# Scores of two head groups on the two halves of TensorE's rows, a first batch attended in halves of its tokens, and casts moved towards ScalarE

## The chip, the core and the metric

The kernel runs on one core of a Trainium2 chip. The metric is the device time in microseconds, taken as the median of several runs. One core has TensorE (PE in the profile, with PEld for its weight loads), VectorE (DVE), ScalarE (ACT), GpSimd (POOL) and SyncE (SP, which issues the transfers here).

## What is computed

Eight batches of eight heads, 576 tokens, head size 64 and 32 memory slots go through a slot attention, and its output goes through two feed-forward layers of 512, 2048 and 512 columns:

```
a = softmax over tokens of phi
k_m, v_m = a^T k, a^T v
scores = q k_m^T / 8, softmax over the 32 slots
x = attn v_m, heads side by side: 4608 x 512
x = (s * relu(x w_in)^2 + b) w_out
out = (h * sigmoid(1.702 h)) w_out2 with h = x w_in2
```

## The kernel before

Each big product is three fp32r matmuls over a high and a low half (`mm3`, L259): `wh*xh`, `wh*xl`, `wl*xh`. So every operand needs a cast to its high half (`hi`, L238, on ScalarE or VectorE, lines L241 and L242 in the profile) and a subtraction for its low half (`lo` and `tt`, L244 to L251, always VectorE, line L247).

The first stage (to about 341 us) works through the batches. For a batch b:

- `slots(b, g)` for the two groups g of four heads: softmax of phi, `k_m` and `v_m` on TensorE (L439, L441), normalised (`norm`, L446) and turned into the tile `km` (L456, then a copy).
- `attend(b, g)`: the scores of one group (L481), eight matmuls into one PSUM tile. Their contraction is 64 rows, `o = slice(64*g, 64*g+64)`, so group 0 uses rows 0 to 63 of TensorE and group 1 rows 64 to 127; their outputs are four strips of 32 columns. Then on VectorE a transposition (L487), the maximum (L500), a subtraction (L490), on ScalarE the exponential (L502), on VectorE sum, reciprocal, product (L494 to L496, L490), a transposition (L505), and the halves `ah` and `al`.
- `matrix(b, j)` for four blocks j of the inner width: `v_m` times `w_in` (L524, 512 columns, both halves of the rows, tile `vw`), with its halves `mh` and `ml`. So the attention weights multiply a folded matrix.
- `step(b, pi, u)`: twelve 128x288 matmuls of `mh`, `ml` with `ah`, `al` for a half u of the tokens (L263 to L265, tile `h`), a relu (L547) and a store.

Batch 0 also converts `w_in` from 64-bit floats (`convert`, L268: five operations on VectorE and ScalarE and one on GpSimd for each of 16 tiles). Batches 2, 3, 4 and 6 carry the preparation of the next layer's weights (`prepare`). The later stages (`down` and `up`) are 8064 more matmuls of 128x288.

The order on every engine is fixed before the run by a list scheduler (`Order`, L28): each operation has a due time and one or two ways (engine, estimated cost). The scheduler takes the way whose start plus `WEIGHT` times cost is least (L115), so `WEIGHT` sets how readily a cast goes to VectorE. Engines run their lists in order. PSUM holds four tiles (`ps`) of two banks each. While `fill` is set, idle TensorE time in the plan is filled with matmuls of an identity (`warm`, L750); the second call of `warm` ends that.

Of the kernel before, what the change touches and what calls it, by code (L numbers as in the profile page):

```python
# [12 lines left out]
F32R = mybir.dt.float32r  # L13
# [5 lines left out]
P = 128  # L19
# [8 lines left out]
class Order:  # L28
# [10 lines left out]
    WEIGHT = {"dve": 1.0, "pool": 1.6, "act": 1.0}  # L39
# [113 lines left out]
class Net:  # L153
# [249 lines left out]
    def slots(self, b, g, due, lead=8):  # L403
# [42 lines left out]
        def norm():  # L446
            s = self.t(rs, [P, 1])
            nc.vector.tensor_scalar(s, T[z][:, 0, 128:129], EPS, None, op0=ALU.add)
            nc.vector.reciprocal(s, s)
            nc.vector.tensor_scalar(self.t(a, [P, P]), T[z][:, 0, 0:128], s, None, op0=ALU.mult)  # L450

        self.on_dve(d + 5, 60, norm, (z,), (a, rs), count=4)
# [10 lines left out]
    def attend(self, b, g, due):  # L463
        nc, T = self.nc, self.T
        S, J = self.S, self.S // 32
        qs = [("t", ("q", b, p)) for p in range(4)]
        if g == 0:
            for p, k in enumerate(qs):
                self.dma(due - 8 + 0.5 * p, lambda k=k: self.t(k, [P, S]), lambda p=p: self.a["q"][b, p], (), (k,))
        d = due  # L470
        ps, sm, sm2 = ((x, ("a", b, g, x)) for x in ("ps", "sm", "sm"))
        sm2 = ("sm", ("a2", b, g))
        st, aT = ("t", ("st", b, g)), ("t", ("aT", b, g))
        km, o = ("km", (b, g)), slice(64 * g, 64 * g + 64)

        def score():
            out = self.pst(ps)
            for u in range(2):
                for p in range(4):
                    w = slice(32 * p, 32 * p + 32)  # L480
                    nc.tensor.matmul(out[w, u, 0:self.HS], T[km][o, w], T[qs[p]][o, u * self.HS:(u + 1) * self.HS], start=True, stop=True)  # L481
# [7 lines left out]
        def with_slots(e, m, op):
            e.tensor_tensor(T[st], T[st], T[m].unsqueeze(2).to_broadcast([P, J, 32]), op=op)  # L490
# [6 lines left out]

        self.pe(d, 2200, score, (*qs, km), (ps,))
        self.on_dve(d + 1, self.HS, turn, (ps,), (st,), count=2)
        self.on_dve(d + 2, S, lambda: nc.vector.tensor_reduce(self.t(sm, [P, J]), T[st], axis=AX.X, op=ALU.max), (st,), (sm,))  # L500
        self.on_dve(d + 2, S, lambda: with_slots(nc.vector, sm, ALU.subtract), (sm,), (st,), port=True)
        self.on_act(d + 3, S, lambda: nc.scalar.activation(T[st], T[st], AF.Exp, scale=0.125), (), (st,))  # L502
        self.on_dve(d + 4, S + 200, total, (st,), (sm2,))
        self.on_dve(d + 4, S, lambda: with_slots(nc.vector, sm2, ALU.mult), (sm2,), (st,), port=True)
        self.on_dve(d + 5, S, lambda: nc.vector.transpose(self.t(aT, [P, S]), T[st].rearrange("p J m -> p (J m)")), (st,), (aT,))  # L505
        ah, al = ("t", ("ah", b, g)), ("t", ("al", b, g))
        self.hi(d + 6, S, lambda: self.t(ah, [P, S], F32R), lambda: T[aT], (aT,), (ah,))
        self.lo(d + 6.5, S, lambda: self.t(al, [P, S], F32R), lambda: T[aT], lambda: T[ah], (aT, ah), (al,))
# [22 lines left out]
    def step(self, b, pi, u, due):  # L531
# [13 lines left out]
        self.pe(due, 12 * HS, mm, (*m, *ats[0], *ats[1]), (h,))  # L545
# [204 lines left out]
    def warm(self, begin):  # L750
# [155 lines left out]
```

## Time and profile before

| | us |
|---|---|
| median of 3 runs (lowest, highest) | 1437.73 (1436.1, 1439.28) |
| the profiled execution, its time | 1438.46 |
| its span | 1436.4 |
| TensorE busy | 1400.5 |
| VectorE busy | 1098.2 |
| ScalarE busy | 762.4 |
| GpSimd busy | 94.7 |

The granted clock over the span is 0.992 of full speed. The time outside the span is 2.1 us. How to read it: busy time of TensorE counts pipelined matmuls as one stretch, so the space from one start to the next tells more than the duration; a row of the timeline has in brackets the idle time before it and what ended that.

### The profile page before, as it was taken

To read this page: it belongs to the slowest core of one execution; us is meant where nothing else is said; L and a number is where in the kernel's file an instruction comes from. 1 tells how busy PE (TensorE), PEld (TensorE's weight loads), DVE (VectorE), ACT (ScalarE), POOL (GpSimd) and SP (SyncE) were. 2 spreads that over 40 slices of the span, in tenths; PEclk is the share of its full clock that TensorE was granted. 3 is DMA by queue.
4 is the path that set the end of the run, shared out by engine and by line. 5 is a ranking of instruction groups with operands and counts; after the bars stand their busy time and mean duration, and the time that the engine had idled before them with its cause. 6 is when DMAs were issued, how large, how long until landed. Compare 5 with 4: busy or idle time off the path is not lost.

```text
span 1436.4 us, 28622 instructions
## 1 busy us (share of the span) xinstructions
PE 1400.5 (98%) x11190; PEld 1340.0 (93%) x11190; DVE 1098.2 (76%) x1728; ACT 762.4 (53%) x1224; POOL 94.7 (7%) x70
## 2 busy tenths in 40 slices
PE   6899999999999999999999999999999999999998
PEld 5778877789999999999999999999999999999998
DVE  7879998986898988898895565752458787777872
ACT  4455654566676666665565555554444434243441
POOL 1400110100101000100110010100000000000000
PEclk9899999999999999999999999999999999999999
DMA  9979999899954465475998756473598433554330
GB/s 354 322 258 340 353 322 344 289 309 366 313 181 131 140 238 149 156 256 171 346 347 318 278 180 239 169 266 133 188 357 310 127 116 108 156 157 131 114 104 34
DMA packets 136775, 329.19 MB, mean 229 GB/s; under 512 B 15552, under 2 KB 15552, under 8 KB 136640
## 3 DMA queue, kind: packets, MB, share of 16 engines
q1 hardware_dynamic: 136640, 327.37, 66.2%
q8 instruction: 88, 1.44, 0.4%
q14 instruction: 47, 0.39, 0.1%
HBM read 192.56 MB, written 134.74 MB: 228 GB/s over the span
## 4 chain that ended last, share of the span: by engine, by line
PE 50%; DMA 1%; DVE 0%; issue 0%; ACT 0%; SPq 0%; DVEq 0%
PE X L611 5%; PE X L613 5%; PE X L612 5%; PE X L718 5%; PE X L720 5%; PE X L719 5%; PE Y L611 3%; PE Y L613 3%; PE Y L612 3%; PE Y L718 2%; PE Y L720 2%; PE Y L719 2%; PE Z L611 1%; PE Z L613 1%; PE Z L612 1%; PE Z L718 1%
## 5 line engine op out<-in xcount | busy, mean ns | idle before, releaser
L263 PE MATMUL h<-ah,mh 128*128 128x288 f32 x512 | 160.5, 313 | 4.7 <-DVE ah L242 4.5
L265 PE MATMUL h<-ah,ml 128*128 128x288 f32 x512 | 154.3, 301 | 9.3 <-DVE ml L247 9.1
L611 PE MATMUL X<-oh,wo 128*128 128x288 f32 x512 | 152.7, 298 | 9.8 <-ACT u L637 9.7
L264 PE MATMUL h<-al,mh 128*128 128x288 f32 x512 | 154.2, 301 | 2.1 <-DVE al L247 2.1
L611 PE MATMUL X<-oh,w 128*128 128x288 f32 x512 | 151.7, 296 | 0.7 <-ACT u L631 0.7
L718 PE MATMUL X<-oh,w 128*128 128x288 f32 x512 | 151.7, 296 | 0.2 <-DMA w<-w 0.2
L612 PE MATMUL X<-ol,wo 128*128 128x288 f32 x512 | 151.6, 296 | 0.0
L719 PE MATMUL X<-ol,w 128*128 128x288 f32 x512 | 151.1, 295 | 0.3 <-DVE ol L247 0.3
L612 PE MATMUL X<-ol,w 128*128 128x288 f32 x512 | 151.0, 295 | 0.0
L613 PE MATMUL X<-oh,wo 128*128 128x288 f32 x512 | 151.0, 295 | 0.0
L720 PE MATMUL X<-oh,w 128*128 128x288 f32 x512 | 150.5, 294 | 0.0
L613 PE MATMUL X<-oh,w 128*128 128x288 f32 x512 | 150.5, 294 | 0.0
L247 DVE TENSOR_TENSOR h<-Y,u 128x576 f32<-128x576 f32 x64 | 48.4, 757 | 128.7 <-ACT u L726 89.5
L547 ACT ACTIVATE r<-h 128x576 f32<-128x576 f32 x122 | 79.5, 651 | 110.2 <-PE h L265 90.8
L263 PEld LDWEIGHTS h<-ah,mh 128*128 128x128 f32 x512 | 99.8, 195 | 26.7 <-ACT r L547 12.0
L247 DVE TENSOR_TENSOR ol<-C,oh 128x576 fp32r<-128x576 f32 x128 | 94.9, 753 | 21.5 <-ACT oh L241 11.4
L265 PEld LDWEIGHTS h<-ah,ml 128*128 128x128 f32 x512 | 99.2, 194 | 10.5 <-DVE ml L247 10.5
L241 ACT CAST oh<-A 128x576 fp32r<-128x576 f32 x106 | 68.1, 672 | 74.3 <-PE Y L613 29.8
L611 PEld LDWEIGHTS X<-oh,wo 128*128 128x128 f32 x512 | 96.2, 188 | 11.7 <-ACT u L637 11.7
L247 DVE TENSOR_TENSOR ol<-A,oh 128x576 fp32r<-128x576 f32 x128 | 94.7, 760 | 15.3 <-PE X L613 5.7
L264 PEld LDWEIGHTS h<-al,mh 128*128 128x128 f32 x512 | 99.2, 194 | 2.9 <-DVE al L247 2.9
L746 ACT ACTIVATE g<-h 128x576 f32<-128x576 f32 x96 | 65.8, 686 | 67.5 <-DVE h L247 64.4
(181 smaller groups left out, 4226.8 us busy)
## 6 DMA issues: line engine op xcount, KB each, us to landing
w<-w SPq DMA_DIRECT2D x112, 512.0 KB, 5.7
r<-r SPq DMA_DIRECT2D x128, 288.0 KB, 4.1
g<-g SPq DMA_DIRECT2D x128, 288.0 KB, 2.7
wo<-wo SPq DMA_DIRECT2D x42, 512.0 KB, 5.2
kv<-in_kv SPq DMA_DIRECT2D x64, 258.0 KB, 4.8
raw<-in_w SPq DMA_DIRECT2D x32, 512.0 KB, 6.1
q<-in_q SPq DMA_DIRECT2D x32, 288.0 KB, 4.9
A<-r SPq DMA_DIRECT2D x32, 288.0 KB, 3.2
```

The lines of the kernel that those rows point to most:

```text
L241: self.order.add(due, [self.act(n, lambda: nc.scalar.copy(out(), src()), psum), self.dve(n, lambda: nc.vector.tensor_copy(out(), src()), f ...
L247: self.order.add(due, [self.dve(n, lambda: nc.vector.tensor_tensor(out(), a(), b(), op=op), port=port)], r, w, first)
L263: self.nc.tensor.matmul(ps, wh, xh, start=start and i == 0, stop=False)
L264: self.nc.tensor.matmul(ps, wh, xl, start=False, stop=False)
L265: self.nc.tensor.matmul(ps, wl, xh, start=False, stop=(i == n - 1))
L547: self.act(2 * HS, lambda: nc.scalar.activation(self.two(r), T[h][:, :, 0:HS], AF.Relu), psum=True),
L611: nc.tensor.matmul(out, T[w][:, 0, c], T[h][:, p], start=f, stop=False, skip_group_check=True)
L612: nc.tensor.matmul(out, T[w][:, 0, c], T[l][:, p], start=False, stop=False, skip_group_check=True)
L613: nc.tensor.matmul(out, T[w][:, 1, c], T[h][:, p], start=False, stop=last, skip_group_check=True)
L718: nc.tensor.matmul(out, T[w][:, 0, c], T[h][:, k], start=f, stop=False, skip_group_check=True)
L719: nc.tensor.matmul(out, T[w][:, 0, c], T[l][:, k], start=False, stop=False, skip_group_check=True)
L720: nc.tensor.matmul(out, T[w][:, 1, c], T[h][:, k], start=False, stop=k == 1, skip_group_check=True)
```

## The change

Scores of both groups of a batch are made in one block, for each half u of the tokens into a PSUM tile of its own, with group 0 and group 1 alternating (`attend`). What follows a score is a function of its own (`weigh`), for one group and either all tokens, `(0, 1)`, or one half of them. Batch 0 is attended in two halves, each with operations of half the length; the other batches in one piece, with the two groups 4 us apart in due time and due where group 0 was. The halves `ah` and `al` get a key for each u. `matrix(0, 0)` is due 16 us sooner, and the filling of TensorE ends when its `ml` and the first half's `al` exist. `norm` leaves its last product to either engine. `WEIGHT` of VectorE goes from 1 to 2.

```diff
-    WEIGHT = {"dve": 1.0, "pool": 1.6, "act": 1.0}
+    WEIGHT = {"dve": 2.0, "pool": 1.6, "act": 1.0}
...
-            nc.vector.tensor_scalar(self.t(a, [P, P]), T[z][:, 0, 0:128], s, None, op0=ALU.mult)
-
-        self.on_dve(d + 5, 60, norm, (z,), (a, rs), count=4)
+
+        def scale(act):
+            x = self.t(a, [P, P])
+            if act:
+                nc.scalar.activation(x, T[z][:, 0, 0:128], AF.Copy, scale=T[rs])
+            else:
+                nc.vector.tensor_scalar(x, T[z][:, 0, 0:128], T[rs], None, op0=ALU.mult)
+
+        self.on_dve(d + 5, 30, norm, (z,), (rs,), count=2)
+        self.order.add(d + 5, [self.act(128, lambda: scale(True), psum=True), self.dve(190, lambda: scale(False))], (z, rs), (a,))
...
-    def attend(self, b, g, due):
+    def attend(self, b, due, groups, apart):
...
+        for n, us in enumerate(groups):
+            d = due + apart[1] * n
+            ps = {u: ("ps", ("a", b, u)) for u in us}
+
+            def score(us=us, ps=ps):
+                for u in us:
+                    out = self.pst(ps[u])
+                    for p in range(4):
+                        w = slice(32 * p, 32 * p + 32)
+                        for g in range(2):
+                            o = slice(64 * g, 64 * g + 64)
+                            nc.tensor.matmul(out[w, g, 0:HS], T[kms[g]][o, w], T[qs[p]][o, u * HS:(u + 1) * HS], start=True, stop=True)
+
+            self.pe(d, 2200 * len(us) // 2, score, (*qs, *kms), tuple(ps.values()))
+            for g in range(2):
+                self.weigh(b, g, us, ps, d, apart[0] * g)
+
+    def weigh(self, b, g, us, ps, d, later):
...
+        n = HS * len(us)
+        J = n // 32
...
+        cols = slice(us[0] * HS, us[0] * HS + n)
...
+            for i, u in enumerate(us):
+                nc.vector.transpose(x[:, i * HS:(i + 1) * HS], T[ps[u]][:, g, 0:HS])
...
+        self.on_dve(d + 1 + 0.5 * g, HS, turn, tuple(ps.values()), (st,), count=len(us))
+        d += later
+        self.on_dve(d + 2, n, lambda: nc.vector.tensor_reduce(self.t(sm, [P, J]), T[st], axis=AX.X, op=ALU.max), (st,), (sm,))
+        self.on_dve(d + 2, n, lambda: with_slots(sm, ALU.subtract), (sm,), (st,), port=True)
+        self.on_act(d + 3, n, lambda: nc.scalar.activation(T[st], T[st], AF.Exp, scale=0.125), (), (st,))
+        self.on_dve(d + 4, n + 200, total, (st,), (sm2,))
+        self.on_dve(d + 4, n, lambda: with_slots(sm2, ALU.mult), (sm2,), (st,), port=True)
+        self.on_dve(d + 5, n, lambda: nc.vector.transpose(self.t(aT, [P, n]), T[st].rearrange("p J m -> p (J m)")), (st,), (aT,))
+        self.hi(d + 6, n, lambda: part(ah), lambda: T[aT], (aT, *made(ah)), keys(ah))
+        self.lo(d + 6.5, n, lambda: part(al), lambda: T[aT], lambda: T[ah][:, cols], (aT, *keys(ah), *made(al)), keys(al))
...
-            self.pe(-5, 0, last, (x, ("t", ("al", 0, 0))))
+            self.pe(-5, 0, last, (x, ("t", ("al", 0, 1), 0), ("w", ("ml", 0, 0))))
...
-                    self.attend(0, g, -28 + 4 * g)
-                self.warm(False)
+                self.attend(0, -28, ((0,), (1,)), (2, 6))
...
-                self.matrix(b, j, d - 8)
+                self.matrix(b, j, d - (24 if b == j == 0 else 8))
+                if b == j == 0:
+                    self.warm(False)
...
-                elif b + 1 < B:
-                    self.attend(b + 1, j - 2, s0 + 18 + 7 * (j - 2))
+                elif b + 1 < B and j == 2:
+                    self.attend(b + 1, s0 + 18, ((0, 1),), (4, 0))
```

What that does to the order is seen at three places. The first is TensorE in batch 0, where `a` is a score's PSUM tile and `km` with two numbers is group 0 and group 1. Before, from the end of group 0's scores through the first half of group 1's:

```order
L481 MATMUL a_268<-q_240,km_202 32x288
L481 MATMUL a_280<-q_194,km_257 32x288
L481 MATMUL a_280<-q_210,km_257 32x288
L481 MATMUL a_280<-q_237,km_257 32x288
L481 MATMUL a_280<-q_240,km_257 32x288
```

Now, the first half of the tokens:

```order
L489 MATMUL a_269<-q_193,km_202 32x288
L489 MATMUL a_269<-q_193,km_256 32x288
L489 MATMUL a_269<-q_209,km_202 32x288
L489 MATMUL a_269<-q_209,km_256 32x288
L489 MATMUL a_269<-q_236,km_202 32x288
L489 MATMUL a_269<-q_236,km_256 32x288
L489 MATMUL a_269<-q_240,km_202 32x288
L489 MATMUL a_269<-q_240,km_256 32x288
```

Neighbours now use different halves of the rows; before, all matmuls of a group used one half.

The second is the end of batch 4's attention for group 1. On VectorE before (`st` is the weights with the slots inside, `aT` their transposition):

```order
L494 TENSOR_REDUCE a_495_2601<-st_2537 128x18
L495 TENSOR_SCALAR a_495_2601<-a_495_2601 128x18
L496 RECIPROCAL a_495_2601<-a_495_2601 128x18
L490 TENSOR_TENSOR st_2537<-st_2537,a_495_2601 128x576
L505 STREAM_TRANSPOSE aT_2612<-st_2537 128x576
L242 CAST ah_2614<-aT_2612 128x576
L247 TENSOR_TENSOR al_2616<-aT_2612,ah_2614 128x576
```

Now on VectorE:

```order
L515 TENSOR_REDUCE a_488_2599<-st_2472 128x18
L516 TENSOR_SCALAR a_488_2599<-a_488_2599 128x18
L517 RECIPROCAL a_488_2599<-a_488_2599 128x18
L511 TENSOR_TENSOR st_2472<-st_2472,a_488_2599 128x576
L537 STREAM_TRANSPOSE aT_2623<-st_2472 128x576
L247 TENSOR_TENSOR ml_2629<-vw_2543,mh_2582 128x1024
L247 TENSOR_TENSOR al_2648<-aT_2623,ah_2631 128x576
```

and on ScalarE, `r` being a step's relu:

```order
L241 CAST mh_2582<-vw_2543 128x1024
L578 ACTIVATE r_2603<-h_2561 128x576
L283 ACTIVATE cwo_2608<-raw_2513 128x512
L578 ACTIVATE r_2625<-h_2584 128x576
L241 CAST ah_2631<-aT_2623 128x576
L578 ACTIVATE r_2644<-h_2610 128x576
```

The cast `ah` went from VectorE to ScalarE, where it stands behind a relu, and an `ml` fills VectorE's list in its place. Over the whole program VectorE's list is 99 instructions shorter (1629 for 1728) and ScalarE's 119 longer (1341 for 1222). In the first stage that is, on VectorE, 12 fewer long `ah` casts, 6 fewer `mh`, 6 fewer relus, 9 fewer `km` copies and 13 fewer products in `norm`; in the later stages some 55 casts `oh`.

The third is VectorE in batch 0 after the scores of batch 1, up to the last `ml` of batch 0 (block j = 3; `an` is a maximum for batch 2's slots). Before:

```order
L413 TENSOR_REDUCE an_819<-ph_632 128x128
L490 TENSOR_TENSOR st_771<-st_771,a_812 128x576
L487 STREAM_TRANSPOSE st_844<-a_821 128x288 x2
L500 TENSOR_REDUCE a_863<-st_844 128x18
L494 TENSOR_REDUCE a_167_869<-st_771 128x18
L495 TENSOR_SCALAR a_167_869<-a_167_869 128x18
L496 RECIPROCAL a_167_869<-a_167_869 128x18
L247 TENSOR_TENSOR ml_885<-vw_835,mh_867 128x1024
```

Now:

```order
L532 TENSOR_REDUCE a_875<-st_830 128x18
L532 TENSOR_REDUCE a_878<-st_835 128x18
L511 TENSOR_TENSOR st_830<-st_830,a_875 128x576
L511 TENSOR_TENSOR st_835<-st_835,a_878 128x576
L413 TENSOR_REDUCE an_913<-ph_657 128x128
L515 TENSOR_REDUCE a_180_929<-st_830 128x18
L516 TENSOR_SCALAR a_180_929<-a_180_929 128x18
L517 RECIPROCAL a_180_929<-a_180_929 128x18
L247 TENSOR_TENSOR ml_937<-vw_902,mh_927 128x1024
```

The second group's maximum and subtraction now stand ahead of that `ml`; before, the second group's subtraction came after it.

## Rows read from the trace of the kernel before

**Rows 1.** The page's first part: busy us, share of the span, instructions.

```profile
PE 1400.5 (98%) x11190; PEld 1340.0 (93%) x11190; DVE 1098.2 (76%) x1728; ACT 762.4 (53%) x1224; POOL 94.7 (7%) x70
```

**Rows 2.** Stretches A:B: length; busy of PE, PEld, DVE, ACT, POOL; PEclk; DMA share; GB/s.

```profile
38.26:81.83 43.57, 41.18 (x372) 33.74 (x373) 38.99 (x70) 21.66 (x33) 14.93 (x11) 0.90 0.92 334
81.83:119.14 37.31, 36.91 (x375) 29.81 (x374) 29.53 (x53) 18.62 (x28) 2.61 (x2) 1.00 0.76 246
...
155.74:192.52 36.78, 36.67 (x375) 29.76 (x374) 35.61 (x63) 24.35 (x38) 5.26 (x4) 1.00 1.00 365
192.52:232.80 40.28, 38.41 (x376) 31.32 (x375) 37.49 (x67) 20.16 (x31) 5.28 (x4) 0.96 0.93 321
232.80:273.24 40.44, 38.60 (x376) 31.29 (x375) 33.17 (x57) 19.34 (x30) 2.62 (x2) 0.96 0.97 338
```

**Rows 3.** Timeline of TensorE: start, us, line, names, rows*columns, shape, count.

```profile
61.66 1.09 PE L524 MATMUL vw<-wi,km 64*32 64x512 f32 x16
62.68 1.09 PE L439 MATMUL s<-kv,ph 128*32 128x129 f32 x32
...
63.95 1.15 PE L481 MATMUL a<-q,km 64*32 64x288 f32 x16
65.03 0.40 PE L263 MATMUL h<-ah,mh 128*128 128x288 f32 x1
```

**Rows 4.** Timeline of TensorE at the start of batch 4.

```profile
195.73 0.40 PE L263 MATMUL h<-ah,mh 128*128 128x288 f32 x1 [1.47 <-DVE ah L242]
196.53 0.40 PE L264 MATMUL h<-al,mh 128*128 128x288 f32 x1 [0.40 <-DVE al L247]
...
197.50 0.44 PE L263 MATMUL h<-ah,mh 128*128 128x288 f32 x1
197.74 0.44 PE L264 MATMUL h<-al,mh 128*128 128x288 f32 x1
...
200.68 0.30 PE L265 MATMUL h<-ah,ml 128*128 128x288 f32 x1
200.81 0.30 PE L263 MATMUL h<-ah,mh 128*128 128x288 f32 x1
```

**Rows 5.** The stretch view just after that, columns as in rows 2.

```profile
196.20:200.20 4.00, 3.67 (x17) 3.67 (x18) 3.86 (x8) 0.65 (x1) 0.28 (x1) 0.60 0.94 293
```

**Rows 6.** VectorE's groups up to 345 us: count, busy us, mean ns, idle before.

```profile
L247 DVE TENSOR_TENSOR ml<-vw,mh 128x1024 fp32r<-128x1024 f32 x32 | 38.8, 1212 | 2.3 <-ACT mh L241 1.8
L490 DVE TENSOR_TENSOR st<-st,a 128x576 f32<-128x576 f32 x32 | 24.2, 758 | 0.8
...
L487 DVE STREAM_TRANSPOSE st<-a 128x288 f32<-128x288 f32 x32 | 13.5, 462 | 3.0 <-PE a L481 3.0
...
L505 DVE STREAM_TRANSPOSE aT<-st 128x576 f32<-128x576 f32 x16 | 12.4, 778 | 0.6
L247 DVE TENSOR_TENSOR al<-aT,ah 128x576 fp32r<-128x576 f32 x16 | 12.1, 757 | 0.5
L500 DVE TENSOR_REDUCE a<-st 128x18 f32<-128x576 f32 x16 | 12.0, 750 | 0.4
L494 DVE TENSOR_REDUCE a<-st 128x18 f32<-128x576 f32 x16 | 11.9, 744 | 1.1 <-ACT st L502 1.1
...
L242 DVE CAST ah<-aT 128x576 fp32r<-128x576 f32 x14 | 6.4, 459 | 0.5
```

**Rows 7.** The same of ScalarE.

```profile
L241 ACT CAST ah<-aT 128x576 fp32r<-128x576 f32 x2 | 1.3, 670 | 0.3 <-DVE aT L505 0.3
```

**Rows 8.** Timeline of VectorE in batch 0.

```profile
22.70 0.85 DVE L487 STREAM_TRANSPOSE st<-a 128x288 f32<-128x288 f32 x2 [0.71 <-PE a L481]
...
36.99 1.22 DVE L247 TENSOR_TENSOR ml<-vw,mh 128x1024 fp32r<-128x1024 f32 x1
...
74.31 1.16 DVE L247 TENSOR_TENSOR ml<-vw,mh 128x1024 fp32r<-128x1024 f32 x1
...
83.35 0.76 DVE L247 TENSOR_TENSOR al<-aT,ah 128x576 fp32r<-128x576 f32 x1
```

**Rows 9.** Timeline of TensorE in batch 0.

```profile
38.26 0.61 PE L265 MATMUL h<-ah,ml 128*128 128x288 f32 x1 [6.53 <-DVE ml L247]
...
53.07 0.40 PE L265 MATMUL h<-ah,ml 128*128 128x288 f32 x1 [2.02 <-DVE ml L247]
```

**Rows 10.** The page's costliest groups: a group of the second stage.

```profile
L611 PE MATMUL X<-oh,wo 128*128 128x288 f32 x512 | 152.7, 298 | 9.8 <-ACT u L637 9.7
```

More of the change, by code (lines that the diff above doesn't have):

```diff
@@ L460, in slots @@
         self.hi(d + 6, 128, lambda: T[km], lambda: T[tr][:, 0, 0:P], (tr,), (km,), psum=True)
-    def attend(self, b, g, due):
-        nc, T = self.nc, self.T
-        S, J = self.S, self.S // 32
+    def attend(self, b, due, groups, apart):
+        nc, T, S, HS = self.nc, self.T, self.S, self.HS
         qs = [("t", ("q", b, p)) for p in range(4)]
[L467 to L481, printed above, removed]
+        kms = [("km", (b, g)) for g in range(2)]
+        for p, k in enumerate(qs):
+            self.dma(due - 8 + 0.5 * p, lambda k=k: self.t(k, [P, S]), lambda p=p: self.a["q"][b, p], (), (k,))
+        for n, us in enumerate(groups):
[12 more added lines that the diff above has]
+                self.weigh(b, g, us, ps, d, apart[0] * g)
@@ L483, in turn @@
+    def weigh(self, b, g, us, ps, d, later):
+        nc, T, HS = self.nc, self.T, self.HS
+        n = HS * len(us)
+        J = n // 32
+        sm, sm2 = ("sm", ("a", b, g, us)), ("sm", ("a2", b, g, us))
+        st, aT = ("t", ("st", b, g, us)), ("t", ("aT", b, g, us))
+        ah, al = ("t", ("ah", b, g)), ("t", ("al", b, g))
+        cols = slice(us[0] * HS, us[0] * HS + n)
         def turn():
             x = self.t(st, [P, J, 32]).rearrange("p J m -> p (J m)")
-            for u in range(2):
-                c = slice(u * self.HS, (u + 1) * self.HS)
-                nc.vector.transpose(x[:, c], T[ps][:, u, 0:self.HS])
@@ L489, in with_slots @@
[L489 to L490 removed]
+            for i, u in enumerate(us):
+                nc.vector.transpose(x[:, i * HS:(i + 1) * HS], T[ps[u]][:, g, 0:HS])
+        def with_slots(m, op):
+            nc.vector.tensor_tensor(T[st], T[st], T[m].unsqueeze(2).to_broadcast([P, J, 32]), op=op)
         def total():
@@ L496, in total, with part, keys, made @@
             nc.vector.reciprocal(m, m)
[L498 to L508, printed above, removed]
+        def part(k):
+            if us[0] == 0:
+                self.t(k, [P, self.S], F32R)
+            return T[k][:, cols]
+        def keys(k):
+            return tuple((*k, u) for u in us)
+        def made(k):
+            return ((*k, 0),) if us[0] else ()
+        self.on_dve(d + 1 + 0.5 * g, HS, turn, tuple(ps.values()), (st,), count=len(us))
[8 more added lines that the diff above has]
+        self.lo(d + 6.5, n, lambda: part(al), lambda: T[aT], lambda: T[ah][:, cols], (aT, *keys(ah), *made(al)), keys(al))
     def matrix(self, b, j, due):
@@ L543, in mm @@
                 self.mm3(out[:, i, 0:HS], [([T[x][:, k, o] for x in m], [T[x][:, c] for x in ats[k]]) for k in range(2)])
-        self.pe(due, 12 * HS, mm, (*m, *ats[0], *ats[1]), (h,))
+        self.pe(due, 12 * HS, mm, (*m, *((*x, u) for k in ats for x in k)), (h,))
         self.order.add(due + 0.5, [
```

## The prediction

> **What bounds it now.** I read the page first: TensorE is busy 1400.5 of 1436.4 us [rows 1], so only what shortens TensorE's own list, or its waits, counts. VectorE's 76% is a mean over stages. The second view is the table of stretches, cut from the same point of one batch to the same point of the next [rows 2]. The undisturbed batches take 37.3 and 36.8 us. Two others take 40.3 and 40.4, with the granted clock down to 0.96. VectorE is busy 35.6 to 37.5 us in a batch where it also prepares weights, so there it is as long as TensorE. Batch 0 takes 43.6. The timeline at the start of batch 4 tells what the 3.5 us are: TensorE waits 1.47 us for the cast `ah` on VectorE and 0.40 for `al` [rows 4]. After that its matmuls start 0.24 us apart (197.50 to 197.74) instead of 0.13 (200.68 to 200.81), with a granted clock of 0.60 over the 4 us from 196.2 [rows 4, 5]. That is the lower of the two levels for most of them, and it loses 0.40 x 4 = 1.6 us. So a wait of 1.9 us costs 3.5.
>
> **Scores on both halves of the rows.** A group's scores are 16 instructions of 288 columns and hold TensorE from 63.95 to 65.03, 1.08 us [rows 3]; two groups take 2.16. `vw`, which already uses both halves of the rows, gets 16 instructions of 512 columns through in 1.02 us (61.66 to 62.68) [rows 3]. At its rate 32 x 288 columns take 1.02 x 9216 / 8192 = 1.15 us. So a batch saves about 1.0. The ends are 0, if alternating halves do not overlap as `vw`'s do, and 1.1, a plain halving. I take 1.0, since `vw` has the same 64-row tiles, column strips and a bank for each half. Of the eight blocks, the first lies in the start-up and batch 1's in batch 0, where VectorE sets the pace; six count: **-6.2 us** (ends 0 and -6.6).
>
> **VectorE relieved in batches 1 to 7.** Off its list go casts of 0.46 us (`ah`), six of `mh` with 1024 columns as long as `ml`'s 1.2 at most, six relus of 576 columns (about 0.76, the length of the `al` row), and short copies [rows 6]. With 20 short ones at about 0.25 that is some 10 x 0.4 + 6 x 1.1 + 6 x 0.7 + 20 x 0.25 = 20 us over seven batches, 2.8 each. VectorE's 37.5 becomes 34.7, while TensorE needs 36.8 - 1.0 = 35.8. So the excess of 3.5 and 3.6 us in batches 4 and 5 [rows 2] should mostly go. It need not all go, since the scores of both groups now come together, and all of the attention must pass VectorE before the next batch starts. By the new order that is 4 score transpositions, 2 maxima, 4 subtractions or products, 2 sums, 2 transpositions, 2 `al` and 2 `ml`: 4 x 0.46 + 2 x 0.75 + 4 x 0.76 + 2 x 0.74 + 2 x 0.78 + 2 x 0.76 + 2 x 1.21 = 13.4 us [rows 6], and up to one more us for other rows in between. TensorE has, from the scores to the next batch, seven steps of 12 x 0.13 = 1.6 and two `vw` of 1.02, 13.2 us, with about half a us for the changes between them and half a us until `al` of group 1 is read; some batches have a step or a `vw` more. These two are level, so I leave waits of 0.5 to 1 us in a few batches, some with a spell of lower clock: **-4.5 us** (ends -7.1, all gone, and 0).
>
> **The cast on ScalarE.** One `ah` takes 0.67 us there for 0.46 on VectorE [rows 6, 7]. The 0.2 us are hidden, since VectorE has the other group's rows or an `ml` to do meanwhile; without that cover two casts cost 0.4 us a batch.
>
> **The start.** The first `ml` is late today: it starts on VectorE at 36.99, and TensorE has waited 6.53 us when it goes on at 38.26 [rows 8, 9]. In the new order 28 transpositions and other short or half-length rows stand between the first transposition (22.70 before [rows 8]) and that `ml`, without the four conversion rows that stood there; I make that 12 us for 14.3, so the first steps start at 34 to 35. But what was put off comes next. To the second `al` of batch 1, at 83.35 [rows 8], VectorE ran with only 3 to 4 us of pauses in 61. The new list up to the same `al` has 112 instructions for 100: the halves add their fixed cost (two transpositions of 288 take 0.85, one of 576 takes 0.78 [rows 6, 8]), and four casts, a copy and a product get away or shorter. The sum is the same within a us. The steps of blocks 1 to 3 wait for `w_in` tiles and `ml` from this list. Then comes a wait that is new: after batch 1's scores the last `ml` of batch 0 now stands behind both groups' transpositions, maxima and subtractions and one maximum of 1.3 us. It was made at 74.31, just in time [rows 8]. By my count it stays at 75 to 76, while TensorE, without the 1.0 of scores and with no transposition between, gets there about 2 us sooner. It waits for that and may lose another 1.6 by the clock. Against it stand the wait of 2.02 at 53.07 [rows 9] and its slow matmuls, which can shrink. I take **+1 us**, with ends -5 (the earlier first steps carry through) and +3.5 (all of that new wait).
>
> **Later stages.** 8064 matmuls keep their order; 57 casts `oh` go to ScalarE. In the second stage TensorE waits 9.7 us for ScalarE's evictions of X [rows 10], and these stand in one list with the casts. I take 0, with ends -4 (the new order puts the evictions earlier) and +6. Nothing is saved there by a lighter VectorE: TensorE does not wait for it.
>
> **Sum.** -6.2 - 4.5 + 1 + 0 = -9.7. The profiled execution took 1438.46, 0.7 above the median of 1437.73. That makes 1428.8 for it, and **1428** for the median.
>
> **Rivals.**
> 1. *The early steps carry through* (the lower end of the start). For it: batch 0 takes 6.3 us more than batch 1 [rows 2], and its matmuls run partly at the lower clock. Against it: VectorE is busy 39.0 of those 43.6 us. 1428 - 6 = 1422.
> 2. *The halves do not overlap*: the scores stay at 2.16. For it: no row shows tiles of both halves in alternation. Against: `vw` [rows 3]. 1428 + 6 = 1434.
> 3. *ScalarE's casts delay the evictions.* A cast of 0.67 us ahead of an eviction is paid in full where TensorE waits for it. If one more stood before each of about nine such evictions, that is 6 us: 1434. For it: the 9.7 us of today [rows 10], which already stand for one late list. Against: the planner ranks evictions ahead. The Trainium skill, "ScalarE: Activation LUTs", section "Rules for kernel authors", says that relu, max, add and multiply belong on VectorE. The casts here agree (0.46 us there for 0.67). By that rule alone the change would be wrong wherever VectorE has room, as in the later stages.
> 4. *Slower: the joint scores choke the batch boundary.* The place is the start of batches 2 to 7. Today group 0's scores come 8 us ahead of group 1's, and half of VectorE's chain is over when the second begins. Now 13.4 us follow one point. If VectorE begins its four transpositions late by 1.5 us, behind a conversion or a maximum of its list, two of the four PSUM tiles stay full for longer and `al` comes 1.5 us after TensorE needs it; with the lower clock 3.1 us a batch. Six batches lose 18.6 instead of today's 7.1, so + 11.5 - 6.2 + 1 = + 6.3: 1444. It decides once the chain from the scores to the last `al` exceeds TensorE's 14.3 us or so. For it: the level count above. Against: 2.8 us less on VectorE in each batch. The Trainium skill, "TensorEngine Tiling (Array Packing)", section "PSUM Bottleneck", warns of this: tiles speed up TensorE but not the emptying of PSUM, which may then be the limit. No row before shows it, as no two score tiles are full together.
>
> **How the numbers follow.** My forecast has 0.60, rival 1 0.12, rival 2 0.05, rival 3 0.11, rival 4 0.12. Within 0.2% means 1434.9 to 1440.6, about what a measurement of this kernel can tell. Faster by more: the forecast almost whole (0.57), rival 1, half of rival 2 and half of rival 3, 0.77. The same: 0.03 of the forecast, the rest of rivals 2 and 3, a little of rival 4, 0.12. Slower: 0.11. The terms' own ends add up to about 1418 and 1438; I leave out the far ends of rivals 1 and 4. The range is 1418 to 1438.
>
> **What would show it.** Right: the joint score block takes 1.1 to 1.2 us; batches 2 to 7 take 36 us each, and the stretches of 40 are gone; the first step starts near 34.5, but batch 1 still starts at 82 to 85; TensorE's waits for X in the second stage remain near 10 us. Wrong: score blocks of over 2 us (rival 2), waits for `al` at every batch's start with the clock down after them (rival 4), batch 1 starting before 80 (rival 1), or waits for X of over 15 us (rival 3).

## The result, and the profile after

The changed kernel takes 1422.38 us (median of 4 runs, 1418.58 to 1423.49), the kernel before 1437.65 in the same comparison: a ratio of 0.9889 with a 95% interval of 0.9868 to 0.991. The forecast was 1428 with a range of 1418 to 1438. The profiled execution, the slowest of the four, took 1423.49 with a span of 1421.4; that is 14.97 less than the 1438.46 of the one before. Below, "the first stage ends" means the start of its last matmul in the timeline of TensorE.

The first part of the page (busy us, share of the span, instructions), to be held against [rows 1]:

```profile
PE 1389.9 (98%) x11214; PEld 1338.5 (94%) x11214; DVE 1053.8 (74%) x1629; ACT 828.5 (58%) x1343; POOL 97.2 (7%) x70
```

VectorE has 44.4 us less to do, ScalarE 66 more, TensorE 10.6 less. Next the view of stretches, cut as in [rows 2] from `vw` to `vw` (batch 0 from 38.26 on, then batches 1 to 6; columns as there):

```profile
38.26:83.00 44.74, 36.89 (x368) 28.33 (x372) 43.48 (x75) 25.30 (x41) 16.34 (x12) 0.98 0.93 330
82.95:117.98 35.03, 35.03 (x375) 29.53 (x375) 24.10 (x43) 21.54 (x34) 3.94 (x3) 1.00 0.79 264
117.98:154.59 36.61, 35.51 (x376) 29.58 (x375) 34.61 (x61) 26.84 (x44) 4.27 (x3) 1.00 0.95 330
154.59:189.55 34.96, 34.96 (x376) 29.42 (x375) 33.28 (x57) 24.21 (x40) 3.94 (x3) 1.00 1.00 376
189.55:224.46 34.91, 34.91 (x375) 29.48 (x375) 33.08 (x57) 23.22 (x38) 4.04 (x3) 1.00 1.00 360
224.46:259.43 34.97, 34.97 (x375) 29.49 (x374) 25.14 (x45) 21.06 (x34) 1.31 (x1) 1.00 1.00 356
259.43:297.50 38.07, 37.31 (x391) 31.14 (x391) 35.50 (x60) 25.81 (x43) 4.00 (x3) 1.00 0.98 344
```

Batches 3, 4 and 5 take 35.0, 34.9 and 35.0 us, where it was 36.8, 40.3 and 40.4; the clock stays at 1.00 through all of them. Batch 6 has 1.8 us of other matmuls in it, before as now. Batch 2 is the odd one, 36.6 as before. Of the kernel before, [rows 2] leaves out two of these stretches, batches 2 and 6:

```profile
119.14:155.74 36.60, 36.53 (x375) 29.78 (x374) 34.13 (x57) 22.59 (x36) 2.97 (x2) 1.00 0.97 340
273.24:312.42 39.18, 38.59 (x391) 31.50 (x390) 36.05 (x63) 21.17 (x34) 2.96 (x2) 1.00 0.79 267
```

The first stage ends at 326.35, where it was 341.27: 14.92 us, the whole of the gain. From there to the end of the last matmul it is 1091.05 us now (1417.40 less 326.35) and 1091.10 before (1432.37 less 341.27).

The scores of one batch in the timeline of TensorE (columns as in [rows 3]), with the `vw` ahead of them and the steps behind:

```profile
103.39 1.09 PE L555 MATMUL vw<-wi,km 64*32 64x512 f32 x16
104.30 1.20 PE L489 MATMUL a<-q,km 64*32 64x288 f32 x32
105.43 0.40 PE L263 MATMUL h<-ah,mh 128*128 128x288 f32 x1
105.66 0.29 PE L264 MATMUL h<-al,mh 128*128 128x288 f32 x1
105.80 0.29 PE L265 MATMUL h<-ah,ml 128*128 128x288 f32 x1
```

The two groups' block starts at 104.30 and the next step at 105.43: 1.13 us, where one group alone took 1.08 [rows 3]. Then the start of batch 4, to be held against [rows 4]:

```profile
189.55 1.09 PE L555 MATMUL vw<-wi,km 64*32 64x512 f32 x16
190.57 0.33 PE L421 MATMUL s<-ident,an 128*128 128x128 f32 x1
190.65 0.38 PE L263 MATMUL h<-ah,mh 128*128 128x288 f32 x1
190.87 0.29 PE L264 MATMUL h<-al,mh 128*128 128x288 f32 x1
191.00 0.29 PE L265 MATMUL h<-ah,ml 128*128 128x288 f32 x1
```

The start of batch 2 in the same view:

```profile
120.43 0.40 PE L263 MATMUL h<-ah,mh 128*128 128x288 f32 x1 [0.70 <-ACT ah L241]
121.22 0.40 PE L264 MATMUL h<-al,mh 128*128 128x288 f32 x1 [0.40 <-DVE al L247]
121.46 0.30 PE L265 MATMUL h<-ah,ml 128*128 128x288 f32 x1
121.59 0.29 PE L263 MATMUL h<-ah,mh 128*128 128x288 f32 x1
```

So at batch 4 nothing is left of the waits of 1.47 and 0.40: after its `vw` the steps follow 0.13 us apart. At batch 2 there are new waits, 0.70 for `ah`, which now comes from ScalarE (ACT), and 0.40 for `al`; behind them the matmuls keep their 0.13 us. Batch 6 has one wait:

```profile
261.80 0.40 PE L265 MATMUL h<-ah,ml 128*128 128x288 f32 x1 [0.76 <-DVE ml L247]
```

Before it was 0.59 at the same place, for the same tile.

The start, against [rows 9]:

```profile
31.55 0.38 PE L263 MATMUL h<-ah,mh 128*128 128x288 f32 x1
31.77 0.29 PE L264 MATMUL h<-al,mh 128*128 128x288 f32 x1
35.69 0.40 PE L265 MATMUL h<-ah,ml 128*128 128x288 f32 x1 [3.62 <-DVE ml L247]
...
47.88 1.09 PE L439 MATMUL s<-kv,ph 128*32 128x129 f32 x32 [2.24 <-ACT ph L425]
...
54.99 0.40 PE L265 MATMUL h<-ah,ml 128*128 128x288 f32 x1 [2.18 <-DVE ml L247]
...
75.28 0.40 PE L263 MATMUL h<-ah,mh 128*128 128x288 f32 x1 [0.31 <-ACT mh L241]
75.51 0.29 PE L264 MATMUL h<-al,mh 128*128 128x288 f32 x1
76.67 0.40 PE L265 MATMUL h<-ah,ml 128*128 128x288 f32 x1 [0.86 <-DVE ml L247]
```

The first step begins at 31.55 and goes on at 35.69 (38.26 before), when the first `ml`, which starts on VectorE at 34.41 (36.99 before), is there. Then come a wait of 2.24 for the exponentials `ph` of batch 1, the old wait of 2 us for `ml`, and the new one for batch 0's last `ml` after the scores of batch 1, 0.86. Batch 1 begins at 82.95, 1.1 later than before. VectorE is busy 43.5 of the 44.7 us of batch 0: it still sets the pace there.

In the later stages the page's group of [rows 10] reads now:

```profile
L642 PE MATMUL X<-oh,wo 128*128 128x288 f32 x512 | 153.3, 299 | 8.6 <-ACT u L668 8.5
```

### The profile page after: what moved, and what is told of

It is laid out like the page before. It is cut to its first block, busy times and chain, and to the rows that moved or that the text cites. A ratio compares the mean times of both kernels' runs of the same rounds, so it can differ in the third digit from the quotient of the medians.

```text
span 1421.4 us, 28723 instructions
## 1 busy us (share of the span) xinstructions
PE 1389.9 (98%) x11214; PEld 1338.5 (94%) x11214; DVE 1053.8 (74%) x1629; ACT 828.5 (58%) x1343; POOL 97.2 (7%) x70
## 4 chain that ended last, share of the span: by engine, by line
PE 91%; DVE 5%; DMA 2%; ACT 1%; issue 1%; SPq 0%; ACTq 0%; DVEq 0%
PE X L642 10%; PE X L644 9%; PE X L643 9%; PE X L749 5%; PE X L751 5%; PE X L750 5%; PE Y L642 5%; PE Y L644 5%; PE Y L643 5%; PE h L263 4%; PE h L265 4%; PE h L264 4%; PE Y L749 2%; PE Y L751 2%; PE Z L642 2%; PE Y L750 2%
## 5 line engine op out<-in xcount | busy, mean ns | idle before, releaser
L263 PE MATMUL h<-ah,mh 128*128 128x288 f32 x512 | 156.9, 306 | 1.1 <-ACT ah L241 0.7
L578 ACT ACTIVATE r<-h 128x576 f32<-128x576 f32 x128 | 83.0, 651 | 59.1 <-PE h L265 46.5
L241 ACT CAST oh<-A 128x576 fp32r<-128x576 f32 x123 | 79.9, 674 | 58.9 <-PE X L643 45.2
L241 ACT CAST oh<-C 128x576 fp32r<-128x576 f32 x115 | 76.6, 673 | 45.5 <-PE Y L643 12.7
```

The source lines that it names most:

```text
L241: self.order.add(due, [self.act(n, lambda: nc.scalar.copy(out(), src()), psum), self.dve(n, lambda: nc.vector.tensor_copy(out(), src()), f ...
L263: self.nc.tensor.matmul(ps, wh, xh, start=start and i == 0, stop=False)
L578: self.act(2 * HS, lambda: nc.scalar.activation(self.two(r), T[h][:, :, 0:HS], AF.Relu), psum=True),
```

## The experiments

All ratios are to the kernel before, measured in the same session on the same chip; "ends" is the end of the first stage in the profiled execution, and "waits for X" the idle time of TensorE in the group of [rows 10]. The rows come from five sessions, in which the kernel before took 1436.7 to 1440.1 us, so two versions are compared by their ratios and not by their medians. "Ends" and "waits" are of one execution each.

| kernel | median us | ratio, 95% interval | ends | waits for X |
|---|---|---|---|---|
| before | 1437.7 | 1 | 341.27 | 9.8 |
| the change | 1422.4 | 0.9889 [0.9868, 0.991] | 326.35 | 8.6 |
| change, WEIGHT 1 | 1435.1 | 0.9979 [0.9958, 1.0] | 339.27 | 10.0 |
| change, scores by group | 1422.7 | 0.9888 [0.9867, 0.9908] | 327.85 | 9.4 |
| before, WEIGHT 2 | 1426.9 | 0.992 [0.9898, 0.9941] | 335.59 | 7.8 |
| joint scores alone | 1431.0 | 0.9945 [0.9924, 0.9966] | 337.25 | 10.0 |
| joint scores and WEIGHT 2 | 1418.9 | 0.9876 [0.9861, 0.9892] | 327.49 | 5.8 |
| change, old start | 1418.8 | 0.9873 [0.9856, 0.989] | 326.50 | 7.5 |
| change, WEIGHT 1 later | 1423.7 | 0.9905 [0.989, 0.992] | 327.39 | 9.4 |
| change, X on VectorE | 1420.9 | 0.9881 [0.9861, 0.9901] | 327.60 | 6.8 |
| change, 4.5 us transfers | 1416.4 | 0.9854 [0.9839, 0.9868] | 325.44 | 4.4 |
| old start, 4.5 us transfers | 1413.8 | 0.9841 [0.9826, 0.9856] | 324.33 | 4.4 |
| 4.5 us, X on VectorE | 1422.6 | 0.9903 [0.9886, 0.9919] | 324.54 | 7.8 |
| old start, 4.5 us, WEIGHT 3 | 1415.4 | 0.9832 [0.9814, 0.985] | 322.87 | 5.8 |

How far one end can be trusted shows in three of the rows. The change, the change with WEIGHT 1 later and the change with X on VectorE have the same lists on TensorE, VectorE and ScalarE up to 308 us, and the first stage ends at 326.35, 327.39 and 327.60. So a difference of about 1.3 us between two ends tells nothing.

### The weight taken back

```diff
-    WEIGHT = {"dve": 2.0, "pool": 1.6, "act": 1.0}
+    WEIGHT = {"dve": 1.0, "pool": 1.6, "act": 1.0}
```

> The changed kernel with VectorE's WEIGHT back at 1 and all else kept. Theory: the waits at the start of batches 4 and 5 (3.5 us each with their slow matmuls) went because casts left VectorE; with the old weight the casts come back, the batches that prepare weights take 37 to 40 us instead of 35.0, and the time is about 1422.4 + 5 = 1427 us. Rival: the joint scores and their earlier due time took those waits away; the batches stay at 35 us and the time at 1422 us.

Measured: 1435.1 us, a ratio of 0.9979 for 0.9889; the first stage ends at 339.27, 12.9 later than with the change. The theory had the direction but less than half of the size (5 us). Without the weight, all the rest of the change keeps 2 us of the 14.9 in the first stage of the profiled execution.

### The order inside a block

```diff
-for p in range(4):
-    w = slice(32 * p, 32 * p + 32)
-    for g in range(2):
-        o = slice(64 * g, 64 * g + 64)
+for g in range(2):
+    o = slice(64 * g, 64 * g + 64)
+    for p in range(4):
+        w = slice(32 * p, 32 * p + 32)
         nc.tensor.matmul(out[w, g, 0:HS], ...)
```

> The changed kernel with the sixteen instructions of a score tile in the other order: group 0's eight and then group 1's eight, so that neighbours use the same half of the rows; nothing else moves on any engine. Theory: the halves overlap only when they alternate, so a block goes from 1.1 to 2.2 us, and seven blocks outside the start give + 7 us: 1430 us. Rival: the gain comes from one block in the place of two (fewer switches on TensorE), and the order inside does nothing: 1422 us.

Measured: 1422.7 us. The theory falls: alternation is not needed. The timelines of TensorE show why. Each row below is the start of a score block, seen through a window that closes shortly after its first instruction, so the count at its end says how many have started by then. The changed kernel, 0.06 us after the first:

```profile
104.30 0.47 PE L489 MATMUL a<-q,km 64*32 64x288 f32 x8
```

This kernel, 0.06 us after the first:

```profile
105.61 0.45 PE L489 MATMUL a<-q,km 64*32 64x288 f32 x8
```

The kernel before, 0.15 us after the first:

```profile
63.95 0.42 PE L481 MATMUL a<-q,km 64*32 64x288 f32 x4
```

In the changed kernel and in this one eight are under way at once, four strips on each half of the rows, whatever their order. Before, four are, all on one half. The gain of the pair comes from the two groups standing next to each other, which before were 6 to 9 us apart.

### The weight alone

In the kernel before:

```diff
-    WEIGHT = {"dve": 1.0, "pool": 1.6, "act": 1.0}
+    WEIGHT = {"dve": 2.0, "pool": 1.6, "act": 1.0}
```

> The kernel before with VectorE's WEIGHT at 2 and nothing else changed. Theory: VectorE's list gets shorter in the batches with preparation, the waits at the start of batches 4 and 5 go (7 us with their slow matmuls): 1437.7 - 7 = 1431 us, and the score blocks stay at 1.08 us each. Rival: the waits went through the joint scores, and the weight alone moves nothing: 1437.7 us; or ScalarE's longer list delays the evictions of X in the second stage: 1440 us.

Measured: 1426.9 us, a ratio of 0.992. The view of stretches for batches 1 to 5, cut from `vw` to `vw` (columns as above):

```profile
84.04:120.67 36.63, 36.63 (x375) 29.73 (x374) 27.93 (x50) 21.16 (x32) 2.63 (x2) 1.00 0.75 249
120.67:157.51 36.84, 36.59 (x375) 29.88 (x374) 32.52 (x57) 25.92 (x42) 5.31 (x4) 1.00 0.95 337
157.51:194.61 37.10, 36.86 (x375) 29.76 (x374) 34.48 (x61) 24.42 (x39) 3.13 (x2) 1.00 0.98 354
194.61:231.20 36.59, 36.59 (x375) 29.71 (x374) 32.72 (x58) 22.73 (x36) 5.31 (x4) 1.00 0.98 355
231.20:268.70 37.50, 36.93 (x375) 29.82 (x374) 28.75 (x50) 22.04 (x33) 1.32 (x1) 1.00 0.99 339
```

The batches of 40 are gone: all five take 36.6 to 37.5 us, with the clock at 1.00, and VectorE is busy 27.9 to 34.5 us in each. Nearly all of what remains is TensorE's own list. In the profiled execution 5.7 us come from the first stage and 4.4 from the later ones (1091.10 to 1086.72), where no term of the theory put anything; the experiment with the weight off in the later stages, below, speaks against a cause in the weight there.

### The joint scores alone

In the changed kernel, with the start of before as well (its diff stands further below):

```diff
-    WEIGHT = {"dve": 2.0, "pool": 1.6, "act": 1.0}
+    WEIGHT = {"dve": 1.0, "pool": 1.6, "act": 1.0}
...
             nc.vector.reciprocal(s, s)
+            nc.vector.tensor_scalar(self.t(a, [P, P]), T[z][:, 0, 0:128], s, None, op0=ALU.mult)
...
-        self.on_dve(d + 5, 30, norm, (z,), (rs,), count=2)
-        self.order.add(d + 5, [self.act(128, lambda: scale(True), psum=True), self.dve(190, lambda: scale(False))], (z, rs), (a,))
+        self.on_dve(d + 5, 60, norm, (z,), (a, rs), count=4)
```

> The joint scores alone: the changed kernel with WEIGHT at 1, the last product of the norm on VectorE, batch 0 attended in one piece, its first matrix due where it was, and the filling of TensorE ended as before. Theory: 1.1 us less in each score pair and some 0.4 for fewer switches, six or seven times, while VectorE is as loaded as before, so that batches 4 and 5 keep waits of 2 to 4 us each: 1437.7 - 9 = 1429 us. Rival 1: the joint order alone takes the waits away too: 1423 us. Rival 2: it chokes the batch boundary without the relief: over 1437 us.

Measured: 1431.0 us. The profiled execution was the slowest of four, 1434.7; in it the first stage ends at 337.25, 4.0 earlier than before. The same view, batches 1 to 5:

```profile
82.78:121.17 38.39, 37.03 (x376) 31.09 (x375) 29.33 (x54) 18.50 (x27) 2.68 (x2) 0.96 0.72 236
121.17:156.65 35.48, 35.27 (x376) 29.59 (x375) 34.46 (x60) 22.77 (x36) 3.01 (x2) 1.00 1.00 363
156.65:192.66 36.01, 35.62 (x375) 29.52 (x374) 34.54 (x64) 24.26 (x38) 5.33 (x4) 1.00 1.00 359
192.66:232.40 39.74, 37.15 (x375) 31.02 (x374) 37.44 (x67) 19.68 (x30) 5.25 (x4) 0.96 0.96 331
232.40:271.42 39.02, 36.77 (x375) 31.10 (x374) 33.47 (x58) 20.16 (x30) 2.86 (x2) 0.96 0.99 343
```

And TensorE's timeline at the starts of batches 4 and 5:

```profile
196.44 0.61 PE L265 MATMUL h<-ah,ml 128*128 128x288 f32 x1 [2.17 <-DVE ml L247]
...
236.20 0.40 PE L265 MATMUL h<-ah,ml 128*128 128x288 f32 x1 [2.25 <-DVE ml L247]
```

Batch 2 takes 35.5, so the saving on TensorE is there. But batches 1, 4 and 5 take 38 to 40, with the clock at 0.96; in 4 and 5 TensorE waits 2.2 us for an `ml` of VectorE, in batch 1 0.97 for `ah` and 0.40 for `al`. In this execution more than half of what the scores gave is waited away. By the medians less is lost: 1431.0 is 8.0 us below the kernel before in the same session.

### Both, and nothing else

In the kernel with the joint scores alone:

```diff
-    WEIGHT = {"dve": 1.0, "pool": 1.6, "act": 1.0}
+    WEIGHT = {"dve": 2.0, "pool": 1.6, "act": 1.0}
```

> The joint scores and WEIGHT 2 and nothing else of the change: the fourth corner beside the kernel before (ratio 1), WEIGHT 2 alone (0.992, first stage ending at 335.6 us) and the joint scores alone (0.9945, first stage ending at 337.3 us). Theory: in the first stage the two need each other, since with joint scores alone TensorE waits for VectorE and with the weight alone nothing is left but TensorE's own list; so the stage ends at 326 to 328 us, 5 us earlier than the two gains added (341.3 - 4.0 - 5.7 = 331.6), and the time is 1419 to 1422 us. Rival: the gains only add, 331.6 us, and the rest of the 14.9 us came from the norm and the split: 1426 us.

Measured: 1418.9 us, and the first stage ends at 327.49, inside the 326 to 328 of the theory. In the profiled executions the two edits alone take 5.7 and 4.0 us off the first stage, together 13.8. But the whole times say otherwise: the two ratios alone multiply to 0.992 x 0.9945 = 0.9866, and together 0.9876 [0.9861, 0.9892] was measured. By these the gains add, as near as the intervals tell. The weight is worth about the same wherever it is put in: 0.992 in the kernel before, 0.993 on top of the joint scores, 0.991 on top of the rest of the change (0.9889 over 0.9979). The profiled execution of the joint scores was the slowest of its four, the one here the fastest of its four. So it is not shown that the two edits need each other. What the norm and the split of batch 0 brought to the first stage, 1.1 us by these ends, is within the scatter.

### The start of before

```diff
-            self.pe(-5, 0, last, (x, ("t", ("al", 0, 1), 0), ("w", ("ml", 0, 0))))
+            self.pe(-5, 0, last, (x, ("t", ("al", 0, 1), 0)))
...
-                self.attend(0, -28, ((0,), (1,)), (2, 6))
+                self.attend(0, -28, ((0, 1),), (4, 0))
+                self.warm(False)
...
-                self.matrix(b, j, d - (24 if b == j == 0 else 8))
-                if b == j == 0:
-                    self.warm(False)
+                self.matrix(b, j, d - 8)
```

> The changed kernel with the start of before: batch 0 attended in one piece, its first matrix due 8 us ahead and not 24, the filling of TensorE ended by the first al. Joint scores, the norm on either engine and WEIGHT 2 stay. Theory (my forecast for the start): the split makes the first steps start 2 to 3 us earlier, but VectorE's list is the same length, so batch 1 starts at the same 82 to 85 us and the time stays at 1422 us, within 1.5. Rival: the early steps carry through, and without the split it is 4 to 5 us slower: 1427 us. Other rival: the split costs time, as the two kernels with WEIGHT 1 hint (1435.1 with it, 1431.0 without): 1418 us.

Measured: 1418.8 us, the number of the second rival. But the interval of its ratio overlaps with that of the change, so the two are not told apart. The first stage ends at 326.50, against 326.35: no difference that an end could show, so the split of batch 0 gained nothing there that can be seen. This kernel and the one with joint scores and WEIGHT 2 differ in the norm alone, and they agree too (0.9873 and 0.9876; 326.50 and 327.49). What this execution took less lies in the second stage, where one wait for X of 1.85 us with its slow matmuls is missing.

### The later stages

```diff
-                    score = t + cost * self.WEIGHT.get(eng, 1.0)
+                    score = t + cost * (1.0 if eng == "dve" and due > self.until else self.WEIGHT.get(eng, 1.0))
```

> The changed kernel with WEIGHT 2 only for what is due in the first stage, and 1 after it. Theory (term 0 for the later stages): TensorE does not wait for VectorE there, the casts can stand on either engine, and the time stays at 1422 us within 2, with TensorE's waits for the evictions of X near 9 us. Rival 1: the 57 casts on ScalarE had delayed the evictions, and without them the waits shrink: 1417 us. Rival 2: the weight alone on the kernel before brought 4 us in the later stages, and this takes them away: 1426 us.

Measured: 1423.7 us, with 9.4 us of waits for X. The casts that moved to ScalarE there cost nothing and bring nothing that can be told from the scatter.

### Evictions of X on VectorE

```diff
-nc.scalar.activation(T[k][:, o], T[X][:, o, 0:HS], AF.Identity, bias=..., scale=self.sc[:, 0:1])
+nc.vector.tensor_scalar(T[k][:, o], T[X][:, o, 0:HS], self.sc[:, 0:1], ..., op0=ALU.mult, op1=ALU.add)
...
```

The reason to try it is ScalarE's timeline in the changed kernel, just ahead of TensorE's wait of 1.85 us that ends at 646.65:

```profile
644.38 0.69 ACT L616 ACTIVATE B<-B 128x576 f32<-128x576 f32 x1 [3.80 <-DMA B<-r]
644.97 0.57 ACT L668 ACTIVATE u<-X,bw,sc 128x288 f32<-128x288 f32 x1
645.45 0.67 ACT L616 ACTIVATE D<-D 128x576 f32<-128x576 f32 x1
646.02 0.58 ACT L668 ACTIVATE u<-X,bw,sc 128x288 f32<-128x288 f32 x1
```

ScalarE stands idle for 3.80 us in front of a square whose load has not come, and the two evictions `u` that TensorE needs stand behind that square and the next one. SyncE had issued that load at 638.30:

```profile
638.30 0.32 SPq L236 DMA_DIRECT2D B<-r  x1
```

In the view of the tile `B` from 630 to 646 us its two transfers take this long from issue to landing:

```profile
DMA to landing us min/median/max: 2.8/4.4/6.1
```

So this one took about 6 us, where the plan reckons 288/340 + 2.0 = 2.85.

> The changed kernel with the second stage's evictions of X (two halves each, scale and bias) on VectorE, in the place of ScalarE. Theory: TensorE waits 8.5 us for them, and 4.4 us go at the lower clock behind those waits, because they stand on ScalarE behind squares whose loads are late (ScalarE waits 3.8 us for one load ahead of the eviction at 645 us); on VectorE they do not stand behind a load, and 5 to 10 us go: 1414 us. Rival: VectorE is 85 to 90% busy in that stage and its list waits for the same loads a little later; the waits come back as waits for VectorE: 1422 us or more.

Measured: 1420.9 us, a ratio that can't be told from that of the change. Of the 6.8 us that TensorE still waits for X, most are now for VectorE's eviction and for a cast on ScalarE. The rival was nearer.

### Transfers planned at 4.5 us

```diff
-            end[n] = t + cost + (2.0 if eng == "sync" else 0.0)
+            end[n] = t + cost + (4.5 if eng == "sync" else 0.0)
```

> The changed kernel whose planner reckons 4.5 us and not 2.0 from the issue of a transfer to its landing (the trace shows 3 to 6 us), in all stages. Theory: the planner then puts evictions of X ahead of squares whose loads have not come, and the waits of the second stage shrink by about half: 1416 us; the first stage may move by some us either way. Rival: the loads are late because SyncE's queue is held up by full tiles, and an order with later loads changes nothing there: 1422 us.

Measured: 1416.4 us. The waits for X are halved:

```profile
L642 PE MATMUL X<-oh,wo 128*128 128x288 f32 x512 | 152.8, 299 | 4.4 <-ACT u L668 4.1
```

The operations are the same, and on balance four of them went from ScalarE to VectorE (1343 to 1339, 1629 to 1633). The mechanism of the theory is seen on ScalarE: from 327 to 700 us it waits some 35 us for loads in the changed kernel and 4.5 us here. Ahead of each of the five waits for X of over 1 us in the changed kernel ScalarE waits for a load, in the 6 us before; ahead of none of the three that are left here (1.16, 1.16 and 1.74). No other value than 4.5 was tried.

### Putting them together

The start of before with 4.5 us transfers:

> The changed kernel with the start of before and with 4.5 us for a transfer in the plan, the two edits that were faster singly (1418.8 and 1416.4). Theory: the start of before was faster only because the order that followed gave one wait fewer in the second stage, and the plan with late transfers already takes that wait away: no sum, 1416 us within 2. Rival: the two add: 1412 us.

Measured: 1413.8 us, the interval of whose ratio lies wholly below that of the change: faster than the changed kernel, and than the one before. Against 4.5 us alone the intervals overlap. By ratios the two single steps would multiply to 0.9838 and 0.9841 was measured, so the rival was nearer; but neither the single gain of the old start nor its gain here is clear of the scatter. The profiled execution gained 1.1 us in the first stage and 1.5 after it against the one with 4.5 us alone.

The evictions on VectorE with 4.5 us transfers:

> The changed kernel with 4.5 us for a transfer in the plan and the evictions of X on VectorE. Theory: of the waits for X that the plan with late transfers leaves (4.1 us and 1.6 of lower clock) about half goes, since ScalarE no longer holds an eviction behind a square: 1414 us. Rival: VectorE's own list makes them late, as in the run with the evictions alone there (waits of 1.2, 1.6, 1.3 and 1.9 us remained): 1416 to 1420 us.

Measured: 1422.6 us, a miss: slower than with 4.5 us alone. The page shows the waits for X back at 7.8 us, 6.1 of them for VectorE:

```profile
L642 PE MATMUL X<-oh,wo 128*128 128x288 f32 x512 | 152.5, 298 | 7.8 <-DVE u L668 6.1
```

The start of before, 4.5 us and WEIGHT 3:

> The fastest version so far (1413.8: joint scores, the start of before, 4.5 us for a transfer in the plan, WEIGHT 2) with WEIGHT 3, which moves still more casts to ScalarE. Theory: from batch 2 on nothing is left of TensorE's waits for VectorE, a batch takes TensorE's own 35.0 us, and more relief brings nothing: the first stage ends at 324 to 325 us and the time stays at 1414 us within 2. Rival 1: batch 0, which still waits 9.7 us for VectorE (5.9 + 2.0 + 1.2 and less), gets faster: 1410 us. Rival 2: ScalarE's list becomes the late one, with waits for ah or mh at the batch boundary: over 1417 us.

Measured: 1415.4 us, in a session in which the kernel before took 1440.1; the ratio of 0.9832 can't be told from the 0.9841 with WEIGHT 2. The first stage ends at 322.87, 1.5 us earlier and a little below what the theory allowed; the wait for the first `ml` falls from 5.9 to 3.9 us. In the profiled execution the later stages took 4.4 us more (1086.83 for 1082.44). Whether more relief still gains anything is not shown.

## Why the prediction held, point by point

**Scores on both halves: -6.2 forecast, some -9.9 found.** The block came out as the sum had it: 1.13 us from its start to the next step for both groups, forecast 1.15. What the term missed is the second interruption that went. In batches without a wait TensorE took 36.6 us before and 34.95 now, 1.65 less and not 1.0. The 0.6 lie, as far as the timelines tell, at the ends of a block: after a score block the first matmul of a step is followed at 0.23 us and not 0.13 (105.43, 105.66, 105.80 above), the entry costs a little too, and the joint block often stands right behind a `vw`, which shares its tiles. The Trainium skill, "TensorEngine Tiling (Array Packing)", section "Key Properties", says that a change of tiling mode drains TensorE; the rows agree in kind, and no run here measured the drain by itself. Six batches of 1.65 make 9.9. The mis-sized step is the count of one block's length without its changes. That neighbours alternate between the halves, as the change writes it, is not needed: standing in one block is enough.

**VectorE relieved: -4.5 forecast, some -6.2 found.** Over batches 1 to 6 VectorE's busy time fell by 20.3 us (206.0 to 185.7), 3.4 a batch (forecast 2.8), and in batch 4 from 37.49 to 33.08. Against a clean batch of 36.6 the six took some 9 us too much before (230.6 - 6 x 36.6 - 1.8 for the other matmuls of batch 6 = 9.2, most of it in 4 and 5); against 34.95 they take 3.0 too much now (214.55 - 6 x 34.95 - 1.8 = 3.0), in batches 2 and 6. The forecast that "it need not all go" held, in these two batches: the waits of batch 2 are new, the one of batch 6 was there before. The mis-sized step is the relief, 2.8 us a batch for 3.4, and with it what was left waiting.

**The sum.** -9.9 - 6.2 + 1.1 - 0.05 is -15.05, against -14.97 measured: both large terms were too small, in the same direction, and the result still lies in the range. The terms were added as if each stood alone. The ratios agree with that (0.9945 and 0.992 singly, 0.9876 together). In the profiled executions it does not (4.0 and 5.7 us in the first stage, 13.8 together), but with a run of the joint scores that was 3.7 us above its median; the record does not settle whether the two help each other. The ends that the prediction gives for its terms add up to about 1415 and 1447, not to 1418 and 1438: its range is narrower than its own ends.

**The start: +1 forecast, +1.1 found.** The first `ml` came earlier, at 34.41 on VectorE, near the counted 34.7 (22.7 + 12), but by luck: the rows ahead of it took 10.65 us and began 1.06 later. What was put off came later. TensorE went on at 35.69 and not at 34 to 35, since the `ml` itself takes 1.2 us more. The new wait for batch 0's last `ml` was 0.86 us with 0.31 for `mh`, and the clock held; at the upper end it could have been 3.5.

**Later stages: 0 forecast, 0.05 found.** The waits for X went from 9.8 to 8.6 us; with more slow matmuls behind them that came out even. That it came out at 0 is partly luck: from one version in the table to the next these stages took 1082.4 to 1092.0 us.

**The rivals.** The early steps did not carry through. The halves do overlap. The evictions were not delayed by the casts: with the casts back on VectorE in the later stages TensorE still waits 9.4 us. The Trainium skill, "ScalarE: Activation LUTs", section "Rules for kernel authors", puts relu and simple arithmetic on VectorE. The weight alone moves relus, and casts with them, the other way, and is worth 0.992: here, where VectorE is level with TensorE, its load decides and not the time of one operation. The choked batch boundary, with waits for `al` at every batch's start, was not seen. Where the joint scores come without the relief, TensorE waits 2.2 us at batches 4 and 5, but for `ml`, in the place of 1.9 before, and the kernel stays faster than before. In the changed kernel 1.1 us of waits are left at batch 2 and 0.76 in batch 6.

**What stays open.** The waits for X in the second stage move by several us from one order to the next (4.4 to 10.0 in the table), and the 4.4 us that the weight alone took off the later stages are in part of that kind (9.8 to 7.8); but for the five of the changed kernel it stays open which instruction decides each of them. What the norm's new way brings is, by the pair of kernels that differ in it alone, too small to be seen.

## What to carry to other kernels

Measure each part of a change alone and all together, and compare whole times of several runs before an interplay is read out of one trace: here single executions said that two edits need each other, while the ratios said that they add. Count a block of small matmuls with its entry and exit: one block in the place of two saved 1.65 us a batch, where its length alone was 1.1. In a list scheduler look first at what it believes of transfers: where an eviction stands behind an operation that waits for a load, a truer landing time in the plan was worth more (a ratio of 0.9889 to 0.9854) than moving the eviction to another engine (0.9881).

## What the runs showed of the hardware that was not expected

Eight score matmuls of 64 rows and 32 columns start within 0.06 us in either order of the halves; the order that the change writes out by hand is not needed. Two transfers of one size differ by more than twofold from issue to landing within 16 us (2.8 to 6.1 us for the loads of `B` above).

Waits at a batch's start do not cost in proportion. At batch 4 before, waits of 1.47 and 0.40 us were followed by a granted clock of 0.60 over 4 us [rows 5]; with the joint scores alone, at batch 1, 0.97 and 0.40 by one of 0.64 (86 to 90 us); at batch 2 now, 0.70 and 0.40 by one of 1.00. In the second stage, after the wait of 1.85 us, the matmuls went mostly at the lower of the two levels again. The stretch view of the changed kernel at both places:

```profile
120.00:124.00 4.00, 3.18 (x22) 2.96 (x23) 3.78 (x6) 3.08 (x5) 0.53 (x1) 1.00 0.86 282
646.20:650.40 4.20, 3.75 (x17) 3.75 (x18) 3.53 (x6) 3.31 (x7) 0.00 (x0) 0.62 0.62 222
```

Why one wait was followed by the lower level and another not, the runs do not settle.
